# Output buffer of the last chunk of an expert layer, a deeper ring for reciprocals, and another queue for the identity matrix

## The chip, the cores and the metric

The kernel runs on one core of a Trainium2 chip. The metric is device time in microseconds (us); before the change three runs gave 619.74, 622.83 and 623.56 us, median 622.83. The core has a matrix engine (PE, with its weight loads shown apart as PEld), VectorE (DVE), ScalarE (ACT), GpSimd (POOL) and SyncE (SP). ACT, SP and POOL can issue DMAs. Each engine runs its own instructions in order; they wait for each other through semaphores.

## The reference

Attention with a learned position bias is followed by two expert layers, all over 4 batches of 576 tokens by 512 channels:

```python
attn = softmax(q @ k.T / 8 + bias(pos));   x = attn @ v          # 4 x 8 heads x 576 x 64
gate = sigmoid(causal_conv5(x, conv_w));   x = (gate * (x @ w_val)) @ w_out      # first expert layer
theta = x @ w_theta;  zr, zi = x * cos(theta), x * sin(theta)                    # second expert layer
u = x + w_tok_r @ zr + w_tok_i @ zi;       out = u + relu(u @ w_ch)
```

## The kernel before, in words

Everything is computed in float32 accuracy: a matmul operand is split into a rounded high part and a low part (`split`, lines 58 to 62: ACT writes the high part, POOL or DVE the low part), and a product is three matmuls (`mm3`, lines 104 to 107).

**Attention** (0 to about 285 us) runs over 80 units. `norm` (line 253) adds a small number to the row sums on DVE (L259), takes the reciprocal into a tile `ri` (L260), and POOL multiplies the exponentials by it (L262). The tiles of pool `sm_p` turn in a ring of six. The transposes of the exponentials (L292) read the identity matrix `idt`, which ACT's queue loads at the start (L1120).

**The first expert layer** works on eight chunks of 288 tokens, c = 0 to 7. `m1_out` (line 557) makes the output of a chunk: per block of 128 channels, twelve matmuls and one ACT instruction (L571) that writes a quarter of an SBUF tile; after the fourth, one DMA (L573) stores the tile to DRAM (`x2d`). For c = 0 to 6 this is the tile `xo`, of which there is one buffer (`bufs=1`), and SP issues the store. For c = 7 it is a tile of the ring `bias` (six buffers, `slab("bias")`, once the bias of the attention), and ACT issues the store.

**The second expert layer** begins when the pools of the first are closed, and its tiles take their memory. The pools' allocator makes a tile wait for whatever last used its bytes. `zc0`, the tile of the first batch's angles, lies on bytes of the `bias` ring. The function `m2` (line 815) is written in the order in which each engine runs it (`manual_schedule`). Its start, for batch b and tile t of 128 tokens, is a pipeline over nine (b, t): `m2_theta_mm` (PE: twelve matmuls of 512 columns, x times w_theta), `m2_turns` (ACT, L626), `m2_fold` (DVE, L631), `m2_trig` (ACT, L637 to L639, with one load of a function table), `m2_x` (PE, four transposes, L645), `m2_z` (DVE, L652; ACT and POOL split the result into `za`). Between them `chan_block` unpacks w_ch (ACT L980 and L990, DVE L984 to L986, POOL L991). `m2_split` splits the x of tiles that `m2_fetch` loads (`xtail` and `xt`, L588 and L584), and theta of (0,4), (1,0) and (1,1) read these splits. `m2_tok` then multiplies by the token matrices (operands `za`, `zb`, `wq`, out tiles `pp`). The tiles `pp` lie on PSUM banks of the thetas, so that they wait for the last of these `m2_fold`, which is (1,1). From there to the end the work is mostly matmuls.

Of the kernel before, what the change touches and what calls it, by code (L numbers as in the profile page):

```python
# [9 lines left out]
F32 = mybir.dt.float32  # L10
# [7 lines left out]
B, H, S, D = 4, 8, 576, 64  # L18
DM = H * D
KC = DM // 128  # L20
HID = 32
NP = H // 2
HALF = S // 2
# [80 lines left out]
def mm3(nc, out, wh, wl, xh, xl, first, last):  # L104
    nc.tensor.matmul(out=out, lhsT=wh, rhs=xh, start=first, stop=False)  # L105
    nc.tensor.matmul(out=out, lhsT=wh, rhs=xl, start=False, stop=False)  # L106
    nc.tensor.matmul(out=out, lhsT=wl, rhs=xh, start=False, stop=last)  # L107


class Kernel:  # L110
# [142 lines left out]
    def norm(self, u):  # L253
        nc = self.nc
        it, qt = self.units[u]
        sm, et, _ = self.sh[it, qt]
        n = 2 if qt < 4 else 1
        ri = self.sm_p.tile([128, 2], F32, tag="ri", name="ri")
        nc.vector.tensor_scalar(out=sm[:, :n], in0=sm[:, :n], scalar1=1e-9, scalar2=None, op0=ALU.add)  # L259
        nc.vector.reciprocal(out=ri[:, :n], in_=sm[:, :n])  # L260
        for e in range(n):
            nc.gpsimd.tensor_scalar(out=et[:, S * e:S * e + S], in0=et[:, S * e:S * e + S], scalar1=ri[:, e:e + 1],  # L262
                                    scalar2=1.0, op0=ALU.mult, op1=ALU.mult)
        if qt == 4:

            nc.gpsimd.tensor_copy(out=et[:, S:S + TT], in_=et[:, 0:TT])
# [290 lines left out]
    def m1_out(self, c, m):  # L557
        nc = self.nc
        b, t0 = c // 2, HALF * (c % 2)
        gvh, gvl = self.m1gv[c]  # L560
        if m == 0:
            if c < 2 * B - 1:
                self.m1o[c] = self.f_p.tile([128, KC, HALF], F32, tag="xo", name="xo", bufs=1)
            else:
                self.m1o[c] = self.slab("bias").bitcast(F32)
        ms = slice(128 * m, 128 * m + 128)
        ps = self.mm_p.tile([128, HALF], F32, tag="mm", name="mm")
        for kc in range(KC):
            mm3(nc, ps, self.wo[0][:, kc, ms], self.wo[1][:, kc, ms], gvh[:, kc], gvl[:, kc], kc == 0, kc == KC - 1)
        xo = self.m1o[c]  # L570
        nc.scalar.activation(out=xo[:, m], in_=ps, func=AF.Copy, scale=0.5)  # L571
        if m == KC - 1:
            (nc.sync if c < 2 * B - 1 else nc.scalar).dma_start(out=self.x2d[b][:, :, t0:t0 + HALF], in_=xo)  # L573
# [497 lines left out]
    def run(self):  # L1071
        tc, nc, a = self.tc, self.nc, self.a
# [7 lines left out]
        def pool(stack, name, bufs=1, side="left", **kw):  # L1080
            return stack.enter_context(tc.tile_pool(name=name, bufs=bufs, side=side, **kw))

        T = dict(reuse_waits="tile")
        with ExitStack() as top:
# [16 lines left out]
            with ExitStack() as att:  # L1101
# [12 lines left out]
                with ExitStack() as bs:  # L1114
                    cst = pool(bs, "b_c", 1, "right")
                    hp = pool(bs, "b_h", cfg["HB"])
                    ep = pool(bs, "b_e", cfg["VB"], "right")
                    pp = pool(bs, "b_p", 2, space=PSUM)
                    self.bias_setup(cst, pp)
                    nc.scalar.dma_start(out=self.idt, in_=a["ident"])  # L1120
                    nc.gpsimd.memset(self.hpi, HPI)
                    nc.gpsimd.memset(self.magic, MAGIC)
                    NG = S // 16
                    pend, loads = [], []

                    def out(n):
                        g, q, ps = pend.pop(0)
                        self.bias_out(g, q, ps, ep)
                        if g % 8 == 7 or g == NG - 1:
                            loads.append((n + cfg["LD"], g // 8))  # L1130

                    for n in range(NG):
                        q = cfg["PAT"][n % len(cfg["PAT"])]
                        pend.append((n, q, self.bias_group(n, q, hp, pp)))
                        if len(pend) > 1:
                            out(n)
                        if n == 6:
                            self.load_qkv(0)
                            self.load_qkv(1)
                        while loads and loads[0][0] <= n:  # L1140
                            self.load_bias(0, loads.pop(0)[1])
                        if n in cfg["S0"]:
                            next(attention)
                    while pend:
                        out(NG)
                    for _, qt in loads:
                        self.load_bias(0, qt)
# [196 lines left out]
```

## Time and profile before

| | us |
|---|---|
| median of three runs | 622.83 |
| the profiled execution | 623.03 |
| its span, first to last instruction | 621.2 |
| PE busy | 587.5 (95%) |
| DVE busy | 494.9 (80%) |
| ACT busy | 412.4 (66%) |

The profiled execution is 0.20 us above the median, and 1.8 us of it lie outside the span. The page cuts the span into 40 slices of 15.5 us; a digit is the busy share of a slice in tenths. The timeline lists instructions by engine, each with the idle time before it and what ended that; a q behind an engine's name marks its sequencer, which issues DMAs. A row "x3" joins three instructions that follow each other.

### The profile page before, as it was taken

The page shows a single profiled execution, that of the slowest core. Times are in us where ns is not written, and L with a number is a line of the kernel's source. Part 1 is how long each engine was busy: PE and PEld are TensorE (multiplying, and loading weights), DVE is VectorE, ACT ScalarE, POOL GpSimd, SP SyncE. Part 2 cuts the span into 40 slices and gives each one's busy share as a digit, 9 for nine tenths or more (in the row PEclk, how much of TensorE's full clock was granted, in tenths as well). Part 3 has the DMA queues.
Part 4 walks back from the last instruction along what each step waited for, and adds up shares of the span by engine and source line. Part 5 has one row for each costly group of instructions (what it writes and reads, how often), then busy time and mean ns, then how long its engine had stood idle before and what let it go on. Part 6 is the DMA issues. An engine that isn't in the chain of part 4 may idle for free. (4 is left out here: it accounts for less than half of the span.)

```text
span 621.2 us, 14621 instructions
## 1 busy us (share of the span) xinstructions
PE 587.5 (95%) x5456; PEld 450.5 (73%) x5456; DVE 494.9 (80%) x1101; ACT 412.4 (66%) x905; POOL 364.5 (59%) x376
## 2 busy tenths in 40 slices
PE   5998999999999998989999999777999999999997
PEld 2333555555555555548899999666999989999997
DVE  7996899999999998768989998199648927955841
ACT  5996877888887988975677765397354256317310
POOL 4563556666665655666589777175648526652641
PEclk9998999999999999999999999977999999999999
DMA  7996699569659963213356336800112402300102
GB/s 186 304 313 200 188 239 264 166 181 244 158 146 247 239 196 99 68 28 100 121 181 188 116 116 215 276 1 0 35 54 79 141 0 73 115 1 26 52 2 76
DMA packets 51270, 84.40 MB, mean 136 GB/s; under 512 B 7168, under 2 KB 32000, under 8 KB 50688
## 3 DMA queue, kind: packets, MB, share of 16 engines
q1 hardware_dynamic: 50384, 82.53, 45.5%
q8 instruction: 43, 0.70, 0.5%
q10 hardware_dynamic: 816, 0.95, 0.4%
q14 instruction: 27, 0.22, 0.1%
HBM read 58.39 MB, written 25.07 MB: 134 GB/s over the span
## 5 line engine op out<-in xcount | busy, mean ns | idle before, releaser
L262 POOL TENSOR_SCALAR e<-e,ri 128x576 f32<-128x576 f32 x144 | 115.1, 809 | 85.3 <-DVE ri L260 42.7
L250 ACT ACTIVATE e<-ns,mx 128x576 f32<-128x576 f32 x144 | 110.7, 771 | 30.6 <-DVE mx L247 15.4
L247 DVE CUSTOM_DVE_ANT_0 ns<-s,bias 128x576 f32<-128x576 f32 x128 | 94.2, 753 | 11.6 <-PE s L233 10.2
L233 PE MATMUL s<-kr,qr 64*128 64x288 f32 (+1 forms) x640 | 93.8, 426 | 0.8 <-DMA kr<-in_k 0.4
L353 PE MATMUL o<-et,vm 128*64 128x320 f32 (+1 forms) x512 | 76.0, 418 | 0.7 <-ACT xst L373 0.7
L62 POOL TENSOR_TENSOR za<-zc,za 128x256 fp32r<-128x256 f32 (+1 forms) x36 | 40.6, 1145 | 49.9 <-ACT za L60 49.9
L292 PEld LDWEIGHTS t<-idt,e 64*128 64x128 f32 x1152 | 42.8, 139 | 36.2 <-POOL e L262 18.9
L233 PEld LDWEIGHTS s<-kr,qr 64*128 64x128 f32 (+1 forms) x640 | 48.1, 179 | 14.7 <-DVE mx L247 5.6
L270 ACT ACTIVATE et<-t 128x512 f32<-128x512 f32 (+1 forms) x103 | 53.8, 545 | 7.4 <-PE s L305 4.9
L353 PEld LDWEIGHTS o<-et,vm 128*64 128x64 f32 x512 | 31.2, 136 | 37.8 <-issue 17.8
L292 PE MATMUL t<-idt,e 64*128 64x64 f32 x1152 | 53.8, 230 | 0.7 <-POOL e L262 0.6
L522 DVE SCALAR_TENSOR_TENSOR gs<-qr,cw,gs 128x288 f32<-128x288 f32 (+4 forms) x96 | 46.2, 512 | 2.8 <-ACT gs L518 2.4
L168 PE MATMUL bp<-h,w2n 128*32 128x512 f32 (+48 forms) x648 | 44.1, 407 | 4.4 <-ACT ev L178 2.4
L155 DVE TENSOR_SCALAR h<-wpsi,nbp_i 128x577 f32<-128x577 f32 (+35 forms) x108 | 45.9, 501 | 0.0
L105 PE MATMUL pp<-wq,za 128*128 128x288 f32 x128 | 39.2, 306 | 3.9 <-DVE zc L631 3.5
L159 POOL TENSOR_SCALAR h<-wpsi,nbp_i 128x545 f32<-128x545 f32 (+11 forms) x12 | 28.7, 2394 | 21.7 <-PE bp L168 15.2
L60 ACT ACTIVATE u<-x 128x288 fp32r<-128x288 f32 x32 | 12.4, 435 | 43.1 <-DVE x L741 39.7
L272 DVE COPY et<-t 128x512 f32<-128x512 f32 (+1 forms) x57 | 35.7, 626 | 6.0 <-PE t L292 4.6
L168 PEld LDWEIGHTS bp<-h,w2n 128*32 128x32 f32 x648 | 16.7, 116 | 31.9 <-ACT ev L178 15.1
L105 PE MATMUL mm<-bias,wo 128*128 128x288 f32 x128 | 38.0, 297 | 1.5 <-DVE gv L554 1.5
L62 POOL TENSOR_TENSOR u<-x,u 128x288 fp32r<-128x288 f32 x32 | 26.2, 840 | 22.2 <-ACT u L60 22.2
L107 PE MATMUL pp<-wq,za 128*128 128x288 f32 x128 | 38.9, 304 | 0.3 <-POOL za L62 0.3
(174 smaller groups left out, 1796.0 us busy)
## 6 DMA issues: line engine op xcount, KB each, us to landing
scr<-ev SPq DMA_DIRECT2D x36, 296.0 KB, 4.5
qr<-in_q SPq DMA_DIRECT2D x32, 288.0 KB, 4.4
bias<-scr SPq DMA_DIRECT2D x32, 288.0 KB, 7.1
vm<-in_v SPq DMA_DIRECT2D x16, 320.0 KB, 5.4
kr<-in_k SPq DMA_DIRECT2D x16, 288.0 KB, 5.1
x<-x2d SPq DMA_DIRECT2D x4, 1152.0 KB, 6.2
out<-o SPq DMA_DIRECT2D x15, 288.0 KB, 2.2
xt<-x2d SPq DMA_DIRECT2D x16, 256.0 KB, 3.3
```

The costliest lines, as they stand in the source:

```text
L62: return a.ins, eng.tensor_tensor(out=lo, in0=src, in1=hi.bitcast(F32), op=ALU.subtract).ins
L105: nc.tensor.matmul(out=out, lhsT=wh, rhs=xh, start=first, stop=False)
L155: nc.vector.tensor_scalar(out=dst, in0=src, scalar1=self.nbp[:, k], scalar2=None, op0=ALU.max)
L168: nc.tensor.matmul(out=ps[32 * c:32 * c + 32, n, o:o + hi - lo], lhsT=self.w2n, rhs=rhs, start=True, stop=True)
L233: nc.tensor.matmul(out=out, lhsT=w, rhs=k[r, e], start=True, stop=True)
L247: self.last_d = nc.vector.tensor_tensor_reduce(out=ns, in0=self.s4[e][:, :, :HALF], in1=bb.rearrange("p (n j) -> p n j", n=2), op0=ALU.add ...
L250: self.last_a = nc.scalar.activation(out=et[:, S * e:S * e + S], in_=ns.rearrange("p n j -> p (n j)"), func=AF.Exp, scale=-1.0, bias=mx[:, ...
L262: nc.gpsimd.tensor_scalar(out=et[:, S * e:S * e + S], in0=et[:, S * e:S * e + S], scalar1=ri[:, e:e + 1], scalar2=1.0, op0=ALU.mult, op1=A ...
L270: self.nc.scalar.activation(out=out, in_=in_, func=AF.Copy)
L292: self.nc.tensor.transpose(out=pt[h][:, 64 * kb:64 * kb + 64], in_=et[r, c:c + 128], identity=self.idt[r, r])
L353: nc.tensor.matmul(out=out, lhsT=vm[:, kb, 64 * e:64 * e + 64], rhs=rhs, start=(kb == 0), stop=(kb == 4))
L522: nc.vector.scalar_tensor_tensor(out=s[:, o:], in0=x[:, o + k:HALF + k], scalar=self.cw[:, m, k:k + 1], in1=s[:, o:], op0=ALU.mult, op1=AL ...
```

## The change

Three edits. The last chunk writes its output into `xo`, as the others do; ACT's queue still issues its store. The tile `ri` gets a ring of twelve. The identity matrix is loaded by POOL's queue instead of ACT's.

```diff
@@ norm @@
-        ri = self.sm_p.tile([128, 2], F32, tag="ri", name="ri")
+        ri = self.sm_p.tile([128, 2], F32, tag="ri", name="ri", bufs=12)
@@ m1_out @@
         if m == 0:
-            if c < 2 * B - 1:
-                self.m1o[c] = self.f_p.tile([128, KC, HALF], F32, tag="xo", name="xo", bufs=1)
-            else:
-                self.m1o[c] = self.slab("bias").bitcast(F32)
+            self.m1o[c] = self.f_p.tile([128, KC, HALF], F32, tag="xo", name="xo", bufs=1)
@@ run @@
-                    nc.scalar.dma_start(out=self.idt, in_=a["ident"])
+                    nc.gpsimd.dma_start(out=self.idt, in_=a["ident"])
```

Behind the second edit the later lines have numbers lower by three in the changed kernel (L571 becomes L568, L626 becomes L623).

ACT at the end of the first expert layer and the start of the second, before (names in brackets are semaphores waited for; DMAHW ones are set by a DMA that lands, and DMAHW2 is here the store of chunk 7):

```order
L96 ACTIVATE wt_4972<-f_6320 128x576 [waits DVE_49]
L571 ACTIVATE bias<-mm 128x288 [waits PE_49] x4
L573 DMA x2d_73<-bias 512x1x288 [waits Activation_49]
L626 ACTIVATE zc_6416<-mm,magic 128x512 [waits DMAHW2_49,Pool_49]
L980 ACTIVATE raw_ch<-raw_ch 128x512 [waits DMAHW5_49]
L980 ACTIVATE raw_ch<-raw_ch 128x512 [waits DMAHW6_49]
L626 ACTIVATE zc_6416<-mm,magic 128x512 [waits PE_49]
```

The same place now:

```order
L96 ACTIVATE wt_4972<-f_6320 128x576 [waits DVE_49]
L568 ACTIVATE xo<-mm 128x288 [waits DMAHW0_49,PE_49,Activation_49]
L568 ACTIVATE xo<-mm 128x288 [waits PE_49] x3
L623 ACTIVATE zc_6416<-mm,magic 128x512 [waits Pool_49]
L570 DMA x2d_73<-xo 512x1x288 [waits Activation_49]
L977 ACTIVATE raw_ch<-raw_ch 128x512 [waits DMAHW4_49]
L977 ACTIVATE raw_ch<-raw_ch 128x512 [waits DMAHW5_49]
L623 ACTIVATE zc_6416<-mm,magic 128x512 [waits PE_49]
```

The first `m2_turns` no longer waits for the store of chunk 7 and stands ahead of it; the first quarter of chunk 7 waits for a DMA that it did not wait for, by the built program's count the store of chunk 6 (DMAHW0). The other numbers of DMAHW semaphores turn by one place, since they are dealt out in turn and one DMA left their circle.

POOL at the start, before:

```order
L1340 UNCONDITIONAL_BRANCH
L1121 MEMSET hpi 128x1
L1122 MEMSET magic 128x1
L159 ISA
L159 TENSOR_SCALAR h_205<-wpsi,nbp_i 128x545
```

and now:

```order
L1337 UNCONDITIONAL_BRANCH
L1117 DMA idt<-in_ident 128x128
L1118 MEMSET hpi 128x1
L1119 MEMSET magic 128x1
L159 ISA
L159 TENSOR_SCALAR h_205<-wpsi,nbp_i 128x545
```

The DMA stands ahead of two small memsets and of POOL's first tile of the bias (L159). On DVE, PE and SP the instructions stand in the same order. On DVE, eighteen of the reciprocals no longer wait for POOL, and nine shifts of the weights' unpacking (L83) now carry a wait for POOL that a reciprocal used to carry.

## Rows read from the trace of the kernel before

**Rows 1.** The page: PE's busy tenths in 40 slices.

```profile
PE   5998999999999998989999999777999999999997
```

**Rows 2.** Waits of ACT from 386 to 428: waiter, releaser, total us, times, longest.

```profile
ACT zc L626 <- DMA x2d<-bias: 9.2, 1, 9.2
```

**Rows 3.** Timeline of PE: start, us, instruction, idle time before it and releaser.

```profile
393.72 0.40 PE L107 MATMUL mm<-wth,xl 128*128 128x512 f32 x1
...
400.00 0.60 PE L645 MATMUL mm<-idt,x 128*128 128x128 f32 x4
406.98 0.80 PE L105 MATMUL mm<-wth,xh 128*128 128x512 f32 x1 [6.38 <-ACT xh L60]
...
427.70 0.61 PE L105 MATMUL pp<-wq,za 128*128 128x288 f32 x1 [3.53 <-DVE zc L631]
```

**Rows 4.** Timeline of ACT.

```profile
389.84 0.99 ACT L571 ACTIVATE bias<-mm 128x288 f32<-128x288 f32 x3
...
391.79 0.59 ACTq L573 DMA_DIRECT2D x2d<-bias  x1
400.99 0.69 ACT L626 ACTIVATE zc<-mm,magic 128x512 f32<-128x512 f32 x1 [9.22 <-DMA x2d<-bias]
...
406.84 0.61 ACT L60 ACTIVATE xh<-xt 128x512 fp32r<-128x512 f32 x1
...
419.69 0.68 ACT L626 ACTIVATE zc<-mm,magic 128x512 f32<-128x512 f32 x1
...
426.26 0.67 ACT L626 ACTIVATE zc<-mm,magic 128x512 f32<-128x512 f32 x1
```

**Rows 5.** Busy us (and count) by stretch: PE, PEld, DVE, ACT, POOL, clock, DMA, GB/s.

```profile
398.00:400.00 2.00, 2.00 (x10) 1.55 (x9) 0.00 (x0) 0.00 (x0) 0.00 (x0) 1.00 1.09 369
...
401.00:423.30 22.30, 15.58 (x68) 12.23 (x68) 19.42 (x28) 22.14 (x41) 15.22 (x14) 0.85 0.01 2
...
428.00:433.00 5.00, 5.00 (x22) 5.00 (x22) 4.74 (x6) 3.03 (x6) 0.79 (x1) 0.50 0.00 0
433.00:440.00 7.00, 7.00 (x54) 7.00 (x54) 5.44 (x8) 4.30 (x6) 2.89 (x2) 0.99 0.18 48
```

**Rows 6.** Timeline of SP's queue.

```profile
386.81 0.57 SPq L573 DMA_DIRECT2D x2d<-xo  x1
...
388.10 1.86 SPq L588 DMA_DIRECT2D xtail<-x2d  x2
390.07 0.58 SPq L578 DMA_DIRECT2D x<-x2d  x1
390.70 1.58 SPq L584 DMA_DIRECT2D xt<-x2d  x2
```

**Rows 7.** DMAs issued at 386.81, 388.10, 390.70, 391.79: KB, us to landing.

```profile
x2d<-xo SPq DMA_DIRECT2D x1, 576.0 KB, 4.2
...
xtail<-x2d SPq DMA_DIRECT2D x1, 128.0 KB, 6.9
...
xt<-x2d SPq DMA_DIRECT2D x1, 256.0 KB, 10.4
...
x2d<-bias ACTq DMA_DIRECT2D x1, 576.0 KB, 9.1
```

**Rows 8.** Timeline of the first 20 us: ACT, POOL and DVE.

```profile
1.16 0.45 ACTq L1120 DMA_DIRECT2D idt<-in_ident  x1
...
5.02 2.67 ACT L157 ACTIVATE h<-wpsi,bp_i 128x577 f32<-128x577 f32 x4 [2.09 <-DVE wpsi L131]
...
5.08 3.09 POOL L159 TENSOR_SCALAR h<-wpsi,nbp_i 128x545 f32<-128x545 f32 x1 [4.24 <-DVE wpsi L131]
...
5.10 15.13 DVE L155 TENSOR_SCALAR h<-wpsi,nbp_i 128x577 f32<-128x577 f32 x32
```

**Rows 9.** Line L260: idle time before it (us, times); line L292: ns, first and last start.

```profile
  DVE sm L259: 0.5, 1
...
L292 PE MATMUL t<-idt,e x1152: 216/223/274, 61.5 to 284.5; 64*128 64x64 f32 x192
```

## The prediction

> **What bounds the kernel now.** I read the page's slices of PE first: behind slice 30 nearly every one is a 9, and the three 7s before, 388 to 435 us, are the place where the second expert layer begins [rows 1]. So I asked for ACT's waits there. One stands out, 9.2 us of the first `m2_turns` (L626) for the store of chunk 7 [rows 2]. The timeline of PE shows what comes of it: PE ends its last free work at 400.6, stands 6.38 us for ACT's split of `xtail`, and later 3.53 us for DVE's last `m2_fold` [rows 3]. The timeline of ACT gives the order in time: the quarters of chunk 7 begin at 389.84, the store is issued at 391.79, L626 starts at 400.99 [rows 4]. From 401.0 to 423.3 ACT is busy 22.14 of 22.30 us [rows 5], and its `m2_turns` of (1,1) at 426.26 is followed by the fold that releases PE at 427.70 [rows 3, 4]. So between 392 and 428 the path is the store, then ACT's own work, then DVE, then PE; PE's 6.38 us lie beside it. Whatever ACT starts earlier at 401 comes off the end, provided that nothing else stops ACT on the way: behind 433 PE is the bound, and its work moves as a whole.
>
> **Chunk 7 into `xo`.** The angles' tile no longer lies on the stored bytes, so L626 loses its wait. Three things follow.
>
> First a new wait: the first quarter of chunk 7 must wait until the store of chunk 6 has read `xo`. That store was issued at 386.81 [rows 6] and took 4.2 us [rows 7]: 391.0. Three quarters took 0.99 us [rows 4], so four from 391.0 end at about 392.3, some 0.5 later than before, when the store was issued behind them at 391.79. On ACT, L626 and the store of chunk 7 stand behind them, so that this store is issued 0.5 to 1 us later too.
>
> Second, L626 starts at 392.3 and not at 400.99. From it to the split of `xt` of (1,0) ACT needed 406.84 - 400.99 = 5.85 us [rows 4]. The inputs are there: theta of (0,1) ends at 394.1 [rows 3], while ACT is at the first L626 and the w_ch work, and the loads of `xtail`, issued by 390.0 [rows 6], took up to 6.9 us [rows 7] and are there by 396.9. The DMA's issue (0.59 us [rows 4]) now falls into this stretch, beside L626 or behind it. ACT would reach the split of (1,0) at 398.2 to 398.8, 8.0 to 8.6 us before 406.84.
>
> Third, what is late next: `xt` of (1,0). Its load was issued at 390.70, behind a load of x [rows 6], and landed 10.4 us later, at 401.1 [rows 7]; the DMA engines were full, 1.09 at 398 to 400 [rows 5]. Before, nobody noticed, since ACT came at 406.84. Now ACT comes at 398 to 399 and stands for 2 to 3 us. With the load landing as before, the split starts at 401.15 and the gain is 406.84 - 401.15 = 5.7 us. The store of chunk 7, in flight at the same time, starts 0.5 to 1 us later and may leave `xt` that much more of the DMA engines: 6.3 us. I take 5.9, nearer to the row as it stands. The ends: 8.6 us if `xt` were there in time, and 3.7 us if it landed 2 us later, about half of the difference between the 9.1 us of chunk 7's store and the 4.2 us of chunk 6's [rows 7].
>
> Behind the split ACT's row is gapless, as before, and it feeds DVE and POOL, so the `m2_turns` of (1,1) and PE's start on `pp` move by the same 5.9 us. The angles of batch 1 now lie on `xo` and wait for the store of chunk 7; their first `m2_turns` stood at 419.69 [rows 4] and would stand at 413.8, while a store issued at about 393 that again takes 9.1 us lands at 402. That hides 11 us. PE's theta of (0,4) follows at once on 400.6, and PE again waits for the last fold, for some 3 us.
>
> **The clock.** In 428 to 433, behind its wait of 3.53 us, PE's granted clock was 0.50, the lower level of 1.2 GHz: 22 matmuls took 5.00 us, where 54 took 7.00 us right behind, at 0.99 [rows 5]. So 22 x (0.227 - 0.130) = 2.1 us are lost on the path. I expect this loss again, since PE stands before `pp` for about as long, with shorter waits ahead of it. If the clock is full there, 2.1 us more are gained; if it stays low for twice as long, 2.1 us are lost.
>
> **The ring of twelve.** The reciprocals waited for POOL's use of a tile six units back. Line 260 shows 0.5 us of idle time in all its instructions, and that for the line before it [rows 9]. The wait cost nothing, so that taking it away gives nothing, and the waits that L83 now carries are for POOL's work on an earlier block of weights. Order and sizes on DVE stay. 0.
>
> **The identity on POOL's queue.** ACT loses 0.45 us of issuing at 1.16, but stands 2.09 us for `wpsi` before its first tile at 5.02 [rows 8]: 0. POOL gets a DMA ahead of two memsets. No DMA of POOL is in this trace, so I bound it: from 0.45 us, ACT's issue of the same load, to the 4.24 us that POOL stands idle before its first tile at 5.08 [rows 8]; any price up to there is hidden. I take the lower end, the row of the same load. `idt` is first read at 61.5 [rows 9], so the transfer's time is hidden too. On SP the third load of q goes out a little earlier, without a stand for another DMA's semaphore, and gains nothing, as SP stands later for ACT anyway. 0.
>
> What could break this is a DMA that POOL cannot start while DVE works: DVE's bias tiles run without a gap for 15.13 us from 5.10 on [rows 8]. SBUF — State Buffer of the Trainium skill (section "SBUF: two separate sides") has this rule: descriptors of a DMA from POOL's queue are written by GpSimd itself, and GpSimd is locked out while VectorE runs in a mode that takes their shared port. No run here shows it yet; without the rule the sum stays as it is, by it the third rival comes in.
>
> **The sum.** 623.03 - 5.9 + 0 + 0 = 617.1 us for an execution like the profiled one, which is 0.20 us above the median of the three runs; I predict 617.0 us.
>
> **The rivals.** (1) More is gained: `xt` lands in time for ACT, or PE's clock is full behind the fold. For it: chunk 7's store comes later, so that loads may come earlier, and PE's wait before `pp` may get shorter. Against it: the DMA engines were full there [rows 5], and have the same bytes to move. It gives 623.0 - 8.6 = 614.4, or 623.0 - 5.9 - 2.1 = 615.0. Chance 0.26.
>
> (2) The wait moves and eats more: the stores of chunks 6 and 7 and `xt` press on each other, ACT stands until 403 or later for `xt`, or the clock stays low for longer. It gives a gain of 1 to 4 us, 619 to 622. In the extreme the edit does nothing at all, if the first quarter of chunk 7 stands until 399.5; but that needs 12.7 us for chunk 6's store in place of 4.2. Chance 0.18.
>
> (3) Slower: POOL's queue is held up by DVE at the start. If the descriptors are not written before 5.10 and have to wait for the end of DVE's 15.13 us, POOL's first bias tile starts at 20.2 and not at 5.08, PE's matmuls of that group stand in order behind it, and with them the whole bias stage: 15.1 - 5.9 = 9.2 us slower, 632 us. It decides from a delay of 4.24 + 5.9 = 10.1 us on. Against it: POOL stands idle for the 4.24 us before 5.08 and has this time for the DMA. Chance 0.05.
>
> (4) The forecast, a gain of 5 to 7 us, 616 to 618. Chance 0.51.
>
> **How the numbers follow.** A measurement of this kernel can tell about 1%, 6.2 us, from no change, so faster begins below 616.6. The forecast lies across that line with its greater part above: I put 0.18 of its 0.51 below. Faster is 0.18 + 0.26 = 0.44, same 0.33 + 0.18 = 0.51, slower 0.05. The three runs of before lie 3.8 us apart, which stays in a median in part. The range takes in the forecast, most of the first rival and the better half of the second: 613.8 to 620.2.
>
> **What would show it.** In the new profile the first quarter of chunk 7 should start at 391, L623 should follow on the quarters at 392 to 393 with no wait for a DMA, and ACT's longest wait there should be for `xt`, 2 to 3 us, ending at 401; PE's wait of 6.38 us should be gone, and the one for the fold should end at 422, with a clock of 0.50 for about 5 us behind it. POOL's first tile should start near 5.1. Were ACT to reach the split of (1,0) at 398.5 without a wait, the sum is too small by 2.5 us; were the split at 404 or later, too great by 3. If all this is so and the time does not move, the path behind 428 was not PE.

## The result, and the profile after

The changed kernel took 614.96 us (median of 16 runs, 613.04 to 620.52) against 621.38 us (16 runs, 618.45 to 626.23) of the kernel before. The ratio is 0.9904, 95% interval 0.988 to 0.9928: some 6.0 us faster, between 4.5 and 7.5. The profiled execution took 613.46 us with a span of 611.7.

The page's row of PE in 40 slices, of 15.3 us now:

```profile
PE   6999999999999998989999999986999999999997
```

Of the three 7s of [rows 1], one 8 and one 6 are left. The timeline of ACT shows what became of the 9.22 us:

```profile
387.53 1.40 ACT L568 ACTIVATE xo<-mm 128x288 f32<-128x288 f32 x4 [0.62 <-DMA x2d<-xo]
388.83 0.68 ACT L623 ACTIVATE zc<-mm,magic 128x512 f32<-128x512 f32 x1
388.96 0.59 ACTq L570 DMA_DIRECT2D x2d<-xo  x1
...
391.32 0.69 ACT L623 ACTIVATE zc<-mm,magic 128x512 f32<-128x512 f32 x1 [0.49 <-PE mm L107]
...
395.00 0.61 ACT L60 ACTIVATE xh<-xtail 128x512 fp32r<-128x512 f32 x1
398.14 0.63 ACT L60 ACTIVATE xh<-xt 128x512 fp32r<-128x512 f32 x1 [2.52 <-DMA xt<-x2d]
...
411.00 0.68 ACT L623 ACTIVATE zc<-mm,magic 128x512 f32<-128x512 f32 x1
...
417.52 0.67 ACT L623 ACTIVATE zc<-mm,magic 128x512 f32<-128x512 f32 x1
```

L623, the first `m2_turns`, follows on the quarters of chunk 7 with no wait. Three smaller waits stand in place of the 9.22 us of [rows 4]: 0.62 us for the store of chunk 6, 0.49 us for PE's theta of (0,1), and 2.52 us for `xt` of (1,0), 3.63 us in all. The first angles of batch 1, which now lie on `xo`, start at 411.00 without a wait.

The clock times can't be compared as they stand, since all of this lies some 3 us earlier. SP's queue gives a mark that the change doesn't touch, the issue of chunk 6's store. Its timeline now, against [rows 6]:

```profile
383.78 0.57 SPq L570 DMA_DIRECT2D x2d<-xo  x1
...
387.57 1.43 SPq L581 DMA_DIRECT2D xt<-x2d  x2
```

This mark moved from 386.81 to 383.78, by 3.03 us. The split of `xt` moved from 406.84 to 398.14, by 8.70. So 8.70 - 3.03 = 5.67 us were gained behind the mark. How long the loads and stores took, from issue to landing, against [rows 7]:

```profile
x2d<-xo SPq DMA_DIRECT2D x1, 576.0 KB, 3.6
x2d<-xo ACTq DMA_DIRECT2D x1, 576.0 KB, 8.9
```

These are the stores of chunks 6 and 7: 3.6 us for the one and 8.9 for the other, which ACT's queue issued while the loads of the second layer were in flight. Chunk 7's store landed at 397.9, 13 us before 411.00. PE's timeline, against [rows 3]:

```profile
405.74 0.50 PE L107 MATMUL mm<-wth,xl 128*128 128x512 f32 x1 [1.03 <-POOL xl L62]
...
413.82 0.40 PE L105 MATMUL pp<-wq,za 128*128 128x288 f32 x1 [1.65 <-ACT za L60]
...
418.97 0.61 PE L105 MATMUL pp<-wq,za 128*128 128x288 f32 x1 [3.54 <-DVE zc L628]
...
423.72 0.30 PE L105 MATMUL pp<-wt,zh 128*128 128x288 f32 x1
```

The wait of 6.38 us is gone, and the one for the last fold is 3.54 us, as long as before (3.53). It ends at 418.97, which was 427.70: 8.73 us earlier, of which 3.03 lie before the mark and 5.70 behind it.

The spans differ by 9.5 us (621.2 and 611.7), so something more was gained. Behind the wait PE runs 24 matmuls on `za` and then the first on `wt`, the last row above. Its row before:

```profile
433.39 0.30 PE L105 MATMUL pp<-wt,zh 128*128 128x288 f32 x1
```

The 24 matmuls took 433.39 - 427.70 = 5.69 us before and take 423.72 - 418.97 = 4.75 now, 0.94 less. From there to the end 0.17 us are lost again: 3.03 + 5.70 + 0.94 - 0.17 = 9.50. The 0.94 us are the clock's. Busy time (and count) of PE, PEld, DVE, ACT and POOL, the granted clock, and DMA, by stretch:

```profile
412.00:417.50 5.50, 1.49 (x8) 0.86 (x6) 5.03 (x8) 4.17 (x8) 4.40 (x5) 0.81 0.00 0
417.50:419.00 1.50, 0.03 (x1) 0.03 (x1) 0.77 (x2) 1.47 (x4) 1.30 (x1) 0.50 0.00 0
419.00:424.00 5.00, 5.00 (x27) 5.00 (x28) 4.74 (x6) 3.03 (x6) 1.06 (x1) 0.67 0.00 0
```

Behind the fold the clock was at its lower level for about two thirds of the first 5 us (0.67), not for all of them (0.50 in [rows 5]). PE got 27 matmuls done there; in the 5 us of [rows 5], which begin 0.3 us behind the end of the wait, it was 22.

The start, against [rows 8]:

```profile
1.23 0.74 POOL L1117 DMA_DIRECT2D idt<-in_ident  x1 [0.80 <-POOLq L1331]
...
4.91 3.09 POOL L159 TENSOR_SCALAR h<-wpsi,nbp_i 128x545 f32<-128x545 f32 x1 [2.79 <-DVE wpsi L131]
```

POOL spent 0.74 us on the identity's DMA, and then still stood 2.79 us before its first tile. Line L260 has no idle time in front of it any more (0.5 us in [rows 9]).

Two questions remain for runs: which edit brought the time, and why ACT gained 5.67 us when it had lost a wait of 9.22.

### The profile page after: what moved, and what is told of

It reads as the page before. It is cut to its first block, busy times and chain, and to the rows that moved or that the text cites. A ratio compares the mean times of both kernels' runs of the same rounds, so it can differ in the third digit from the quotient of the medians.

```text
span 611.7 us, 14609 instructions
## 1 busy us (share of the span) xinstructions
PE 584.1 (95%) x5456; PEld 447.3 (73%) x5456; DVE 493.4 (81%) x1101; ACT 412.7 (67%) x905; POOL 363.6 (59%) x377
## 5 line engine op out<-in xcount | busy, mean ns | idle before, releaser
L292 PEld LDWEIGHTS t<-idt,e 64*128 64x128 f32 x1152 | 43.0, 140 | 36.6 <-POOL e L262 19.1
L292 PE MATMUL t<-idt,e 64*128 64x64 f32 x1152 | 54.0, 231 | 0.7 <-POOL e L262 0.6
L159 POOL TENSOR_SCALAR h<-wpsi,nbp_i 128x545 f32<-128x545 f32 (+11 forms) x12 | 27.0, 2250 | 22.8 <-PE bp L168 18.1
L105 PE MATMUL pp<-u,wv 128*128 128x288 f32 x128 | 38.8, 303 | 0.0
```

The source lines that it names most:

```text
L292: self.nc.tensor.transpose(out=pt[h][:, 64 * kb:64 * kb + 64], in_=et[r, c:c + 128], identity=self.idt[r, r])
```

## The experiments

**Which of the three edits.** Three runs make one edit each on the kernel before. The chunk alone:

```diff
@@ m1_out, on the kernel before @@
-            if c < 2 * B - 1:
-                self.m1o[c] = self.f_p.tile([128, KC, HALF], F32, tag="xo", name="xo", bufs=1)
-            else:
-                self.m1o[c] = self.slab("bias").bitcast(F32)
+            self.m1o[c] = self.f_p.tile([128, KC, HALF], F32, tag="xo", name="xo", bufs=1)
```

> The kernel before with the second edit alone: chunk 7 writes xo. Theory (the whole gain is ACT's wait for the store, cut short by the wait for xt): ratio to before 0.990 (0.988 to 0.993), the same as with all three edits; from chunk 6's last quarter to the split of (1,0) some 5.7 us less than before, with a wait for xt of about 2.5 us ahead of that split. Rival (the identity or the ring carry the 2.8 us by which the changed kernel's trace leads ahead of 380 us): ratio 0.994 to 0.996, and no lead ahead of 380 us.

Measured: 614.81 us against 620.86, ratio 0.9903 (0.987 to 0.9936). That is the whole gain. The timeline of ACT:

```profile
388.15 1.32 ACT L568 ACTIVATE xo<-mm 128x288 f32<-128x288 f32 x4 [1.10 <-DMA x2d<-xo]
...
398.29 0.63 ACT L60 ACTIVATE xh<-xt 128x512 fp32r<-128x512 f32 x1 [2.40 <-DMA xt<-x2d]
```

The waits for the store of chunk 6 and for `xt` are there again, 1.10 and 2.40 us. The mark, chunk 6's store, stands at 383.94 here, so that the split comes 14.35 us behind it, where it was 20.03 before (406.84 - 386.81): 5.68 us. The clock gave nearly nothing back in this trace: the 24 matmuls behind the fold's wait take 5.52 us (419.12 to 424.64).

The identity alone:

```diff
@@ run, on the kernel before @@
-                    nc.scalar.dma_start(out=self.idt, in_=a["ident"])
+                    nc.gpsimd.dma_start(out=self.idt, in_=a["ident"])
```

> The kernel before with the third edit alone: the identity loaded by POOL's queue. Theory: nothing is waiting for it, ratio 1.000 (0.997 to 1.003), the 9.2 us wait of ACT at the start of the second layer stays. Rival (the lead ahead of 380 us comes from here, from the first loads or the semaphores that turn): ratio 0.995 to 0.997. Third rival of the prediction (POOL held up by DVE): first tile of POOL at 10 us or later, ratio above 1.005.

Measured: 621.62 us, 1.0017 (0.9991 to 1.0043). No change.

The ring alone:

```diff
@@ norm, on the kernel before @@
-        ri = self.sm_p.tile([128, 2], F32, tag="ri", name="ri")
+        ri = self.sm_p.tile([128, 2], F32, tag="ri", name="ri", bufs=12)
```

> The kernel before with the first edit alone: a ring of twelve for ri. Theory: the wait for POOL six units back never ended last, ratio 1.000 (0.997 to 1.003), line 260 shows no more than 0.5 us of idle time as before. Rival (the ring carries the lead ahead of 380 us): ratio 0.995 to 0.997, and the units from 60 to 280 us run 2 to 3 us quicker.

Measured: 619.56 us, 0.9978 (0.9953 to 1.0004). The interval takes in no change, by a hair.

**Is the load of xt what takes back the rest?** The changed kernel, with the two loads of `xt` issued ahead of the load of x of batch 1 (1152 KB) and not behind it:

```diff
@@ m2, on the changed kernel @@
         self.m2_fetch(0, 4)
+        self.m2_fetch(1, 0)
+        self.m2_fetch(1, 1)
         self.m2_load(1)
...
-        self.m2_fetch(1, 0)
...
-        self.m2_fetch(1, 1)
```

> The changed kernel with the loads of xt of (1,0) and (1,1) issued ahead of the load of x of batch 1 instead of behind it. Theory (what is late next is xt): xt of (1,0) lands some 4 us earlier, ACT's 2.5 us wait for it goes, and the split of (1,0) comes 2.5 us earlier: ratio to before 0.986 to 0.987, some 2.5 us under the changed kernel. Rival (POOL or DVE end last behind the split, or PE's clock eats it): the split moves by 2.5 us, PE's start on pp by less than 1, ratio 0.989 to 0.991.

Measured: 612.12 us, 0.9855 (0.9819 to 0.989), beside 0.9904 of the change. ACT's timeline:

```profile
394.78 0.62 ACT L60 ACTIVATE xh<-xtail 128x512 fp32r<-128x512 f32 x1
395.30 0.62 ACT L60 ACTIVATE xh<-xt 128x512 fp32r<-128x512 f32 x1
```

The split of `xt` follows at once on that of `xtail`. The mark is at 383.51, so the split comes 11.79 us behind it, 2.57 us sooner than with the change (398.14 - 383.78 = 14.36). Its windows behind the fold, which here ends a wait of 3.53 us at 416.15:

```profile
411.00:416.00 5.00, 1.30 (x6) 0.83 (x6) 3.97 (x7) 3.64 (x7) 3.83 (x5) 0.86 0.00 0
416.00:421.00 5.00, 4.85 (x20) 4.85 (x21) 4.74 (x6) 3.02 (x6) 1.25 (x1) 0.50 0.00 0
```

So `xt` was what ACT stood for. From its split to the end of the fold's wait it takes 20.85 us here, 20.83 in the change and 20.86 before, so that what ACT gains reaches this point whole. The kernel of e1 ran on the same chip: 614.26 to 616.25 us, where this one took 611.58 to 612.49, so 2.7 us of gain in the medians.

At the end of the two traces less is left, 0.7 us (610.7 - 383.51 and 611.7 - 383.78). The clock lost again what it lost before the change, 20 matmuls in 4.85 us at 0.50. And 44 us behind the fold ACT waits for the `xt` of a later tile, here and in the change:

```profile
460.38 0.63 ACT L60 ACTIVATE xh<-xt 128x512 fp32r<-128x512 f32 x1 [3.28 <-DMA xt<-x2d]
```

```profile
461.26 0.63 ACT L60 ACTIVATE xh<-xt 128x512 fp32r<-128x512 f32 x1 [2.46 <-DMA xt<-x2d]
```

It waits 0.82 us longer in e4, and some 10 us behind it PE has fallen back by the same 0.8 us. So with the first `xt` in time, a later one takes back a part.

**Is it the shared DMA engines or the order of the queue?** On the kernel before, the 1152 KB load was taken out of the way of chunk 7's store: ACT's queue issues it, behind the first `m2_turns`.

```diff
@@ m2, on the kernel before @@
-        self.m2_load(1)
...
+        self.x2[1] = self.x2_p.tile([128, KC, S], F32, name="x2", tag="x2")
+        self.nc.scalar.dma_start(out=self.x2[1], in_=self.x2d[1])
```

> The kernel before, its chunk 7 still in the bias ring, with one load moved: x of batch 1 (1152 KB) is issued by ACT behind the first m2_turns, so behind the landing of chunk 7's store, and no longer ahead of it. Theory (the 9.1 us of that store were queueing behind the loads of x, and ACT's wait for it was the loss): the store lands some 4 to 5 us sooner, L626 starts near 396 instead of 401, and the time falls by 3.5 to 5 us, ratio 0.992 to 0.995, without the edit of the change. Rival (the store itself takes 9 us, from the ACT queue or this tile): L626 stays at 401, ratio 1.000.

Measured: 619.42 us against 621.53, 0.9967 (0.9945 to 0.999): about 2 us, less than expected. Two rows of its answers on DMA:

```profile
x2d<-bias ACTq DMA_DIRECT2D x1, 576.0 KB, 6.3
xt<-x2d SPq DMA_DIRECT2D x2, 256.0 KB, 6.4
```

The store of chunk 7 took 6.3 us and not 9.1 [rows 7], and `xt` 6.4 and not 10.4, with the 1152 KB out of the way. ACT's L626:

```profile
396.53 0.69 ACT L626 ACTIVATE zc<-mm,magic 128x512 f32<-128x512 f32 x1 [6.41 <-DMA x2d<-bias]
```

It starts 11.83 us behind the mark (384.70), where it was 14.18 before: 2.35 us gained, and the time agrees. So about a third of the store's 9.1 us came from one load that stood ahead of it. SP issued that load and ACT the store, so it wasn't the order within one queue; the DMA engines that both used were full from 398 to 400 us in the kernel before (1.09 [rows 5]). For `xt`, which SP issues behind that load, this run can't tell the two apart. What the rest of the 9.1 us comes from is not shown: the other loads (x of batch 0, `xtail`, `xt`) were still ahead of the store, and chunk 6's store, issued ahead of them all, took 4.2 us [rows 7].

**The clock behind the fold.** In the kernel of e4 the first token product of batch 0 is now computed twice into the same tile. These 24 matmuls more leave the output as it is; they stand where PE waits for the fold.

```diff
@@ m2_tok, on the kernel of e4 @@
-            for j in range(4):
+            for j in [*range(4)] * (2 if b == 0 and name == "p1" else 1):
```

> The kernel with xt loaded first, and the first token product of batch 0 computed twice into the same tile (24 matmuls more), in the time in which PE waits for the last fold. Theory of the clock term (PE's idle time ahead of the fold brings the lower clock, which costs 2.1 us behind it): the wait of 3.5 us is filled, the granted clock stays near 1.0 behind the fold, and the time falls 1.5 to 2.1 us under the kernel with xt first, ratio to before 0.982 to 0.983, with more work. Rival (the clock falls anyway, or DVE ends last behind the fold): same time as with xt first, 0.985 to 0.987, or 1 to 3 us more if the second copy itself runs at the lower clock and ends behind the fold.

Measured: 609.44 us, 0.9809 (0.9781 to 0.9838). Its windows:

```profile
411.00:416.00 5.00, 4.39 (x30) 4.03 (x30) 3.95 (x7) 3.67 (x7) 3.83 (x5) 1.00 0.00 0
416.00:421.00 5.00, 4.61 (x35) 4.51 (x35) 4.74 (x6) 2.97 (x6) 1.60 (x1) 1.00 0.00 0
```

PE does 30 matmuls where it did 6 in e4, the clock stays at its upper level, and behind the fold 35 matmuls pass where 20 did. The end of the fold's wait and the first matmul on `wt` in e6, and the latter in e4:

```profile
416.49 0.40 PE L105 MATMUL pp<-wq,za 128*128 128x288 f32 x1 [0.39 <-DVE zc L628]
...
419.77 0.30 PE L105 MATMUL pp<-wt,zh 128*128 128x288 f32 x1
```

```profile
421.79 0.30 PE L105 MATMUL pp<-wt,zh 128*128 128x288 f32 x1
```

The wait ends 32.63 us behind the mark (383.86), as in e4 (416.15 - 383.51 = 32.64). The 24 matmuls behind it take 3.28 us, where they took 5.64 in e4: work that nobody needs gained 2.36 us in the trace. The medians give 0.9855 - 0.9809 = 0.46%, 2.9 us, somewhat more than expected, but each was measured against the kernel before on another chip, and their intervals overlap.

**The rule on POOL's DMA.** In the change the DMA runs at 1.23, before DVE's bias tiles, so that its trace can't test the third rival. Here POOL issues it behind its second bias tile, while DVE works on its own:

```diff
@@ run, on the kernel before @@
-                    nc.scalar.dma_start(out=self.idt, in_=a["ident"])
...
+                            with tc.issue_after(self.pool_h):
+                                nc.gpsimd.dma_start(out=self.idt, in_=a["ident"])
```

> The kernel before with the identity loaded by POOL's queue, behind POOL's second bias tile, at 12 to 13 us, in the middle of DVE's gapless bias work; one look at the length of POOL's DMA instruction and its landing. By the rule of the page SBUF of the Trainium skill (GpSimd is locked out while VectorE holds the shared port) the issue takes several us or lands late. Rival (DVE's operations leave POOL enough room): about 0.8 us of POOL and 4 us to landing, as in the changed kernel at 1.2 us. The time of the kernel should not move by either.

POOL's and DVE's rows of its timeline:

```profile
7.48 10.65 DVE L155 TENSOR_SCALAR h<-wpsi,nbp_i 128x561 f32<-128x561 f32 x23
...
12.34 0.84 POOL L1138 DMA_DIRECT2D idt<-in_ident  x1
```

DVE runs these 23 tiles, part of a row of 33, without a gap from 7.48 to 18.13, and in the midst of them POOL's DMA takes 0.84 us, 0.10 more than in the change, and lands after 4.1 us (3.9 there). One run gave 622.62 us, inside the spread of the kernel before. DVE held up neither the issue nor the transfer.

**Do ring and identity count once the rest is out of the way?** First the kernel of e6 with the ring of six and the identity on ACT's queue, and, with the edit of e3, the ring alone again:

```diff
@@ on the kernel of e6 @@
-        ri = self.sm_p.tile([128, 2], F32, tag="ri", name="ri", bufs=12)
+        ri = self.sm_p.tile([128, 2], F32, tag="ri", name="ri")
...
-                    nc.gpsimd.dma_start(out=self.idt, in_=a["ident"])
+                    nc.scalar.dma_start(out=self.idt, in_=a["ident"])
```

> The kernel with xt first and the first token product twice, with the ring of six and the identity on ACT's queue as before: of the change only chunk 7 in xo is left. Theory (ring and identity are worth nothing): ratio to before 0.981, within 0.002 of the kernel with all edits. Rival (the ring is worth the 1.4 us that its single run hinted at): ratio 0.983 to 0.984.

> The ring of twelve alone once more, since its first ratio, 0.9978 with an interval of 0.9953 to 1.0004, left 1.4 us open. Theory: ratio 1.000, with an interval that holds 1. Rival (the ring is worth 1 to 2 us): ratio 0.997 to 0.998 again, and an interval below 1.

Measured: 611.87 us, 0.987 (0.9831 to 0.9909), and 620.84 us, 0.9989 (0.9968 to 1.0011). The second is no change. The first lay 0.6% above e6, and in its trace the granted clock was 0.75 and 0.76 in two stretches of the attention; that of the kernel before has 0.70 and 0.80 there:

```profile
53.00:56.00 3.00, 2.83 (x48) 1.16 (x48) 0.00 (x0) 1.70 (x3) 1.17 (x2) 0.75 0.51 135
56.00:60.00 4.00, 3.98 (x44) 1.74 (x34) 1.22 (x3) 2.44 (x4) 0.00 (x0) 0.76 0.67 208
```

The traces of e6 and of the change show 1.00 there. So the two edits were undone one by one, on one chip with the kernel of e6 again (e10):

```diff
@@ e11, on the kernel of e6 @@
-                    nc.gpsimd.dma_start(out=self.idt, in_=a["ident"])
+                    nc.scalar.dma_start(out=self.idt, in_=a["ident"])
@@ e12, on the kernel of e6 @@
-        ri = self.sm_p.tile([128, 2], F32, tag="ri", name="ri", bufs=12)
+        ri = self.sm_p.tile([128, 2], F32, tag="ri", name="ri")
```

> The kernel of e6 once more (loads of xt ahead of x, first token product computed twice, ring of twelve, identity on POOL's queue), as the mate of the two that follow. Theory: ratio to before 0.981, as e6 gave, within 0.003. If e6 was lucky with its low-clock stretches in the attention, it comes out nearer to e8's 0.987.

> e10 with the identity on ACT's queue again. Theory: the identity's queue is worth nothing, ratio of e10 within 0.002. Rival: with the identity on ACT's queue a stretch at a granted clock of 0.5 appears near 54 us (as in the traces of before, e8 and e9), all later times are 1.6 to 2.6 us late, and the ratio lies 0.003 to 0.004 above e10's.

> e10 with the ring of six for the reciprocals again. Theory: the ring is worth nothing, ratio of e10 within 0.002. Rival: the ring is what made e8 slower than e6, and the ratio lies 0.004 or more above e10's.

Measured against 621.43 us: e10 609.94 us, 0.9812 (0.9777 to 0.9847), e6 once more; e11 610.08 us, 0.9816 (0.9777 to 0.9855); e12 613.14 us, 0.9854 (0.9814 to 0.9893). The identity's queue is worth nothing. The low clock in the attention isn't its doing either, since e11 has the identity on ACT's queue and this row:

```profile
53.00:56.00 3.00, 3.00 (x55) 1.38 (x46) 0.77 (x2) 2.14 (x3) 0.26 (x1) 1.00 0.88 240
```

Nor is it the ring's: the trace of e12, with six, has 1.00 in these two stretches, and that of e9, with twelve, 0.67 and 0.82.

The ring stays open. On the kernel before and in the change it gives nothing that can be told from zero: 0.22% (e3), 0.11% (e9), and 0.01% lost in the change beside e1 (which differ by the identity too). On the kernel of e6 it looks otherwise. There e12 lies 0.42% above e10, 2.6 us, and on that one chip five of its six executions (611.86 to 614.81 us) lie above all twelve of e10 and e11 (608.79 to 611.73). The traced execution of e12 was its fastest (609.58 us), so that no trace shows what the others lost. Their mean granted clock was 0.988 to 0.997, in the traced one 1.000, in e10 and e11 0.993 to 1.000. So in that kernel the ring of twelve may be worth 2 or 3 us; how it would gain them isn't shown.

## Why the prediction was right, point by point

**The wait moved, as forecast.** The edit on chunk 7 alone gave the whole difference (e1), and its mechanism is in the rows: no wait at the first L623, a short one at the first quarter, one of 2.52 us for `xt`, and 3.5 us for the fold, as long as before. Set back by the 3.03 us of the mark, the prediction's times are these: first quarter 391.0 - 3.0 = 388.0 (was 387.53), L623 392.3 - 3.0 = 389.3 (388.83), ACT ready for (1,0) at 395.2 to 395.8 (395.62, 2.52 before 398.14), `xt` there at 398.1 (398.14), end of the fold's wait 421.8 - 3.0 = 418.8 (418.97). Each is within half a microsecond. One input was not there as I had it: ACT stood 0.49 us for theta of (0,1), and the wait for `xt` hid that.

**The term of 5.9 us** measured 5.67. The row as it stands had given 5.7; the 0.2 us that I added, for a store of chunk 7 that would leave `xt` more of the DMA engines, did not come: the store was issued 5.18 us behind the mark (388.96), and 4.98 before (391.79 - 386.81), so it did not come later by the 0.5 to 1 us that I took. Chunk 6's store had landed in 3.6 us, 0.6 sooner than before. `xt` landed 14.3 us behind the mark in both traces, so the second rival, in which the stores and `xt` press on each other, did not come in either.

**What was late next** was named rightly, and e4 prices it: with `xt` in time, 2.57 us more at the split. The upper end of 8.6 us would have been 5.67 + 2.57 = 8.24. Of the first rival's two reasons, `xt` in time did not come about in the change itself, and a full clock behind the fold came in part.

**The clock.** I expected the loss of 2.1 us again. Beside the 3.28 us that the 24 matmuls behind the fold take in e6 at the upper level, the kernel before lost 2.41 us, e1 2.24, e4 2.36, and the change's profiled execution 1.47. So the loss came again in e1 and e4, as forecast, and in the change's own trace 0.94 us of it (2.41 - 1.47) did not. What the executions without a trace lost isn't shown. I had seen rightly that PE's wait before `pp` keeps its length.

**Ring and identity at 0.** The identity holds (e2, and e11 beside e10). POOL's DMA cost 0.74 us of its time and not the 0.45 that I took, far below the 4.24 at which it would show. For the ring, e3 and e9 hold on the kernel before, and so does the change beside e1; e12 speaks against a 0 in the kernel of e6.

**The third rival** did not come in, and the reason that I gave against it, POOL's idle time before 5.08, held: the DMA ran there. e7 shows more, that DVE's bias tiles don't hold up POOL's DMA even beside them. What failed in the rival as I had built it is the hold until the end of DVE's whole row: 23 tiles took 10.65 us, 0.46 each, and POOL's DMA was through within two of them. SBUF — State Buffer of the Trainium skill (section "SBUF: two separate sides") has GpSimd locked out while VectorE is in a mode that takes the shared port, for the whole of that instruction. The trace shows at most a hold of 0.10 us (0.84 and 0.74), less than one tile; whether these tiles run in such a mode no run here shows.

**The number.** I predicted 617.0, and 614.96 was measured, 2.0 us below. Of this, 622.83 - 621.38 = 1.45 us is the starting point: the median of the three runs shown lay above that of the 16. The rest, 0.6 us, is the gain in the medians, 6.4 us, against the 5.8 from 622.83 to 617.0. So the gain is that of the forecast, 5 to 7 us, while the time lies outside its 616 to 618 and at the 615.0 of the first rival. The latter is chance: it comes from the starting point, and not from a full clock.

In the two profiled executions the difference is larger, 9.57 us, since the one of before was late by 3.03 us at the mark already. Of these, 2.5 us stand at 61 us: the first matmul of L292 starts at 61.5 before [rows 9] and at 59.0 in the change, behind the stretch from 53 to 60 us in which the clock was 0.70 and 0.80 before. Nothing shows that the change does this. Of e3 and e9, which are one kernel, only e9 has the low stretch in its trace (0.67 and 0.82). The mark stands from 382.70 (e3) to 387.58 (e7) in the traces without the edit on chunk 7, and from 383.33 (e10) to 385.93 (e8) in those with it. A reader who compares the traces end to end would have found 3 us of gain too many.

## What to carry to other kernels

A tile that waits for a DMA of something unrelated is worth a look at who used its bytes before; here moving one output out of the way gave 6.0 us. Price such a wait not at its length (9.22 us) but at what comes late next on the same engine: the load behind it let 5.67 us through, and putting that small load ahead of a large one gave 2.57 more there, 2.7 in the time. Compare two traces from a mark just ahead of the change, never from zero.

## What was not expected of the hardware

The same wait of PE, 3.53 or 3.54 us, was followed by 5 us at the lower clock in the kernel before and in e4, and by about 3.3 of 5 us in the changed kernel. There the clock had fallen earlier: it was at its lower level in the whole of 417.5 to 419 and, at a mean of 0.81, for about 2.1 us of the 5.5 us before, in which PE had done 8 matmuls. That is 3.6 us ahead of the end of the wait, where it fell 1.4 us ahead of it in the kernel before (the clock of 426 to 427 us was 0.63, and 1.00 up to 426). The loss behind a wait thus varied by nearly 1 us at an equal wait, with where in the wait the clock fell; what set this moment isn't shown. And it paid to give PE something to do in such a wait: 24 needless matmuls brought e6 2.36 us in its trace, with the clock at its upper level throughout. e6, with the three edits, the order of loads of e4 and these matmuls, is the fastest version: 609.44 and, again, 609.94 us.
